# Attention and mixer kernel: weight and second-batch loads in one run on POOL ahead of casts, v's shifted copies on VectorE, first lists rearranged

## The chip, the cores and the metric

The kernel runs on one core of a Trainium2 chip. The metric is the device time of one execution in microseconds (us), of which several runs are taken. Engines are called as in the profile: PE (TensorE, matmuls), DVE (VectorE), ACT (ScalarE), POOL (GpSimd) and SP (SyncE, which here only issues DMAs). PE's clock is granted by a throttle; the profile gives it as a share of full speed.

## The reference

Eight batches, eight heads, 576 positions, 64 elements a head. First attention with a window of 32 to either side and 8 global positions, which see and are seen by all; then a mixer over tokens (576 to 256 and back) and one over channels (512 to 1536 and back).

```python
scores = scale * np.matmul(q, k.transpose(0, 1, 3, 2))
mask = np.abs(pos[:, None] - pos[None, :]) <= window
mask = mask | is_global[:, None] | is_global[None, :]
scores = np.where(mask, scores, -1000000000.0)
attn = softmax(scores)          # row maximum taken off, sum + 1e-09
x = np.matmul(attn, v)          # heads side by side: B, S, 512
xt = x.transpose(0, 2, 1)
h = np.maximum(xt @ w_tok1, 0.0) @ w_tok2
u = x + h.transpose(0, 2, 1)
h2 = np.maximum(u @ w_ch1, 0.0) @ w_ch2
return u + h2
```

## The kernel before

**Stages of a batch.** q and k come in as float32 (`lq`, `lk` for the first 512 positions, `lqr`, `lkr` for the last 64) and are cast to float16 (`cast_qk`, L384 and L381). PE transposes them (`T`, L398, and `TR`, L425), and DVE copies the result out of PSUM (`TEq`, `TEk`, L404 and L410; `TRE`, L436). `S_` (L456) makes the scores in the window, `SX` their exponentials on ACT (L468), `SM` the masks on DVE (L474, L479). `GK`, `LX`, `LM` serve the global keys, `OG` (with the DVE result `rf`, L542) the global queries. `PV` multiplies by v (L654, L663) and divides by the row sums (L676, L677), giving `x16s`. `M1` and `M2` (L690, L710) are the token mixer; `M3` transposes u by DMA (`uT`, L727; for the last tile `uTl`, L730). `M4` (L738) and `M5` (L764) are the channel mixer: 12 and 8 units of about 0.87 and 1.3 us per batch. An output tile `osb` (L768) is added on DVE and sent by SP (L769).

**Shifted copies.** A tile of v holds 128 positions, a query tile 64. So there is a second copy of v, shifted by 64 rows (`vod`, made by `v_odd`, L371 and L372: two copies over 64 partitions). For batch 0, v arrives in float32 (`lv`) and is cast by POOL (`castv`, L376); later batches are loaded and cast at once by five DMAs from POOL (`load_v16`, L359).

**Order.** All engines' orders are those of the program. There is no automatic scheduling. Batch 0's attention and token mixer come from a list written out by hand at the end of the function (L882 to L1016), in which the weight loads (`load_w1`, L247, `load_w1l`, `load_w2`, `load_wc1`, `load_wc2`, L263; float32 to float16, so all on POOL) and the loads of batch 1's q and k (`load_qk1`, on POOL too) are placed. After that, period b runs the dense units (`M4`, `M5`) of batch b, with the sparse work of batches b+1 and b+2 between them. In period 0 the list is `period_0` (L821 to L835): a `D` in it stands for one dense unit. Period 1 merges the list of `sparse2` (L779) with the dense units by planned durations; from period 2 on `first_half` and `second_half` repeat. 

**Queues.** SP's queue holds batch 0's q, k and v, the outputs, the transposes and the q and k loads of batch 2 and on (`load_rest`, L120, `load_qk`, L116), in that order of issue: a load behind an output waits until that output's tile is there. In `period_0` of before, the loads for batch 2 stand ahead of batch 1's last masks and its `OG`. POOL's queue holds, for batch 1, the casts of q and k, `v_odd(1)`, and the gathers of the global rows.

**Buffers.** q, k (float16), v, `vod` and the transposed q and k are double, by b % 2; `lq` and `lk` are single, so their loads wait for the casts of the batch before. PSUM has three pools: `pss` (two buffers), `psv` (one), `psm` (two, also of the dense units).

Of the kernel before, what the change touches and what calls it, by code (L numbers as in the profile page):

```python
# [15 lines left out]
P = 128  # L16
# [28 lines left out]
def kernel(  # L45
# [72 lines left out]
    def load_rest(b):  # L118
        for ten, dst in ((q, lqr), (k, lkr)):
            (nc.scalar if b == 0 and ten is q else nc.sync).dma_start(out=dst.rearrange("p i d -> p (i d)"), in_=rest_src(ten, b))  # L120
# [12 lines left out]
    for p in range(NP):  # L133
        load_qk(0, slice(2 * p, 2 * p + 2))
        if p == 0:
            load_rest(0)
        if p == 2:
            load_v0(0)
# [19 lines left out]
    def qk_pads(i):  # L158
        nc.gpsimd.memset(kTs[i][:, :, 0:WIN], 0.0)
        nc.gpsimd.memset(kTs[i][:, :, WIN + S :], 0.0)  # L160

    qk_pads(0)
    nc.gpsimd.memset(qTs[0][:, :, :, 0:NG], 0.0)
# [113 lines left out]
    nc.gpsimd.memset(lv[0:WIN, 0], 0.0)  # L277
    nc.gpsimd.memset(lv[P - WIN : P, NT - 1], 0.0)
# [10 lines left out]
    def v_rows(i):  # L289
        nc.gpsimd.memset(vsh[i][0:WIN, 0], 0.0)  # L290
        nc.gpsimd.memset(vsh[i][P - WIN : P, NT - 1], 0.0)
# [102 lines left out]
    def T(b, p):  # L394
        pT = (psm if b == 0 else pss)([P, 2, 512], F16, name=f"pT_{b}_{p}")
# [23 lines left out]
    def TR(b):  # L419
        pr = (psm if b == 0 else pss)([P, 2, 4, NP * 16], name=f"pr_{b}")  # L420
# [85 lines left out]
    def GK(b):  # L506
        s = st[b]
        ps = (psv if b == 0 or b > 2 else pss)([P, 2, 512], name=f"gk_{b}")
# [23 lines left out]
    def OG(b):  # L532
        s = st[b]
        ps = (psv if b > 2 else pss)([P, 2, VW], name=f"og_{b}")
# [13 lines left out]
    def OG0(p):  # L548
        s = st[0]
        if p == 0:  # L550
# [48 lines left out]
    def M1_0(p):  # L599
        s = st[0]  # L600
        if p == 0:
# [43 lines left out]
    def PV(b, tau):  # L645
# [4 lines left out]
        ps = (pss if b > 2 and tau % 2 else psv)([P, 2, 512], name=f"pv_{b}_{tau}")  # L650
# [128 lines left out]
    def sparse2():  # L779
# [7 lines left out]
        for p in range(NP):  # L787
# [33 lines left out]
    def period_0():  # L821
# [6 lines left out]
        u += [D, lambda: SM(n, 2), lambda: GK(n), s2(n, 3), D, lambda: (load_rest(m), load_qk(m, slice(0, H)))]  # L828
        u += [lambda: SM(n, 3), D, lambda: OG(n), D, lambda: PV(n, 0), D, lambda: PV(n, 1), D]
        u += [lambda: PV(n, 2), lambda: [M1(n, ch) for ch in range(2)], lambda: PV(n, 3), D]  # L830
        u += [lambda: PV(n, 4), lambda: M1(n, 2), D, lambda: [M1(n, ch) for ch in range(3, NT)], *c2]
        u += [lambda: (M2(n, 0), M3(n, 0)), lambda: (M2(n, 1), M3(n, 1)), lambda: (M2(n, 2), M3(n, 2))]
        u += [lambda: (load_v16(m), v_odd(m)), lambda: globals_(m), lambda: TR(m)]
        u += [lambda p=p: t(m, p) for p in range(NP)]
# [46 lines left out]

    W(10)  # L882
    indices()
    W(20)
    consts()
    cast_qk(0, 0, 0, A)
    cast_qk(0, 1, 0, A)
    cast_qk(0, 0, None, V)
    T(0, 0)
    gather(0, (1,))  # L890
    masks_c()
    TEq(0, 0, V)
    TEk(0, 0, A)
    cast_qk(0, 0, 1, A)
    cast_qk(0, 1, 1, V)
    S_(0, 0, 0)
    SX(0, 0, 0)
    gather(0, (0,))
    v_ones(0)
    v_rows(0)  # L900
    nc.gpsimd.memset(w1l, 0.0)
    T(0, 1)
    cast_qk(0, 0, 2, V)
    masks_b()
    TEk(0, 1, A)
    TEq(0, 1, A)
    cast_qk(0, 1, None, A)
    S_(0, 1, 0)
    cast_qk(0, 1, 2, G)
    TR(0)  # L910
    masks_d()
    SX(0, 1, 0)
    G(out=g16[1][0], in_=g32[1][0])
    T(0, 2)
    TRE(0, (1,), V)
    TRE(0, (0,), A)
    castv(0)
    S_(0, 1, 1)
    TEq(0, 2, V)
    TEk(0, 2, A)  # L920
# [3 lines left out]
    G(out=g16[0][0], in_=g32[0][0])  # L924
    load_w1()
    load_w1l()
    load_w2()
    cast_qk(0, 1, 3, V)
    gather_t(0)
    SX(0, 0, 1)  # L930
    S_(0, 2, 0)
    GTE(0)
    GKE(0)
    T(0, 3)
    SX(0, 2, 0)
    v_odd(0, slice(0, 2), nc.vector)
    S_(0, 2, 1)
    TEk(0, 3, A)
    TEq(0, 3, V)
    SX(0, 2, 1)  # L940
    GQ0()
# [116 lines left out]
```

The softmax here doesn't subtract the row's maximum and nothing guards it: scores larger than these inputs give would overflow.

## Time and profile before

| | us |
|---|---|
| median of 5 runs | 351.67 |
| lowest and highest run | 349.37 and 352.43 |
| the profiled execution | 348.58 |
| its span | 346.7 |
| PE busy | 310.5 (90%) |
| DVE busy | 187.5 (54%) |
| ACT busy | 154.0 (44%) |
| POOL busy | 95.9 (28%) |

The lines shown below are from one profiled execution. The span is what the trace covers; the execution's own time is some 2 us longer. The mean granted clock was 0.984. Numbers such as L398 are lines of the kernel before; a bracket at the end of a line tells how long the engine stood idle just before and what ended that.

Two lines of the page show where PE is less than busy, in 40 slices of 8.67 us:

```profile
PE   5599689783999999799989999899989999999993
DMA  7899959999939873948194914968101221052012
```

A digit is the busy share in tenths (9 stands for 90% or more). PE's low digits are nearly all in the first ten slices, that is in the start-up and in period 0; the DMA engines are nearly full in the first slices.

### The profile page before, as it was taken

How to read it: one execution, taken by the hardware profiler on the slowest of the kernel's cores; microseconds unless marked ns; L12 is line 12 of the kernel's file. 1: busy time of each engine (PE TensorE's matmuls, PEld its weight loads, DVE VectorE, ACT ScalarE, POOL GpSimd, SP SyncE). 2: the span in 40 equal slices, each digit the busy share in tenths (PEclk: the TensorE clock that was granted, in tenths of full speed). 3: DMA queues.
4: the chain of work that ended last, by engine and by line, in shares of the span. 5: the costliest groups of instructions: out<-in, count | busy, mean ns of one | idle time of the engine just before them, and what ended most of it. 6: DMA issues, size and time to landing. Idle time of an engine off the chain costs nothing.

```text
span 346.7 us, 8081 instructions
## 1 busy us (share of the span) xinstructions
PE 310.5 (90%) x3431; PEld 166.8 (48%) x3431; DVE 187.5 (54%) x380; ACT 154.0 (44%) x276; POOL 95.9 (28%) x125
## 2 busy tenths in 40 slices
PE   5599689783999999799989999899989999999993
PEld 5368344432346544444445644454545545444641
DVE  5588166548653875576647464566656364231021
ACT  4554463042757145463465444554555433403600
POOL 8995292856415101520052002510000000000000
PEclk9699999999899999999999999999999999999999
DMA  7899959999939873948194914968101221052012
GB/s 219 195 149 225 230 78 149 300 144 121 228 82 89 253 173 47 87 151 223 70 97 121 218 62 79 85 211 169 62 2 30 62 93 33 0 119 79 0 74 80
DMA packets 82022, 42.37 MB, mean 122 GB/s; under 512 B 56578, under 2 KB 76674, under 8 KB 81986
## 3 DMA queue, kind: packets, MB, share of 16 engines
q1 hardware_dynamic: 43944, 31.20, 33.2%
q0 software_dynamic: 37904, 10.52, 28.8%
q8 instruction: 27, 0.44, 0.5%
q10 hardware_dynamic: 138, 0.13, 0.1%
q14 instruction: 9, 0.07, 0.1%
HBM read 36.11 MB, written 9.44 MB: 131 GB/s over the span
## 4 chain that ended last, share of the span: by engine, by line
PE 69%; DMA 11%; DVE 8%; POOL 6%; issue 2%; SPq 1%; ACT 1%; POOLq 0%; ACTq 0%
PE op L764 25%; PE b1p L738 20%; DMA lk<-in_k_dram 6%; PE a1p L690 4%; PE hp L710 4%; PE pv L654 3%; PE b1lp L751 3%; PE pv L663 2%; PE s L456 2%; DMA vsh<-in_v_dram 2%; PE pT L398 2%; DMA uT<-u 1%; DVE x L677 1%; DVE e_all L479 1%; DMA lv<-in_v_dram 1%
## 5 line engine op out<-in xcount | busy, mean ns | idle before, releaser
L738 PE MATMUL b1p<-uT,wc 128*128 128x512 f16 x384 | 95.9, 383 | 2.1 <-DMA uT<-u 2.1
L741 ACT ACTIVATE b<-b1p 128x512 f16<-128x512 f32 x96 | 57.0, 598 | 91.4 <-PE b1p L738 91.3
L764 PE MATMUL op<-wc,b 128*128 128x512 f16 x384 | 89.8, 380 | 0.0
L468 ACT ACTIVATE e_all<-s 128x544 f16<-128x544 f32 (+1 forms) x64 | 41.2, 687 | 40.2 <-issue 32.3
L359 POOL DMA_DIRECT2D vsh<-in_v_dram x35 | 29.5, 862 | 98.3 <-PE pv L663 91.3
L764 PEld LDWEIGHTS <-b 128*128 128x128 f16 x384 | 35.2, 98 | 38.9
L738 PEld LDWEIGHTS <-wc 128*128 128x128 f16 x384 | 34.4, 98 | 39.0 <-issue 4.0
L768 DVE TENSOR_TENSOR osb<-u,op 128x512 f32<-128x512 f16 x32 | 22.0, 687 | 54.4 <-PE op L764 52.2
L404 DVE COPY qT<-pT 128x512 f16<-128x512 f16 x31 | 21.3, 687 | 15.4 <-PE pT L398 15.3
L479 DVE TENSOR_TENSOR e_all<-e_all,bandm 128x616 f16<-128x616 f16 x56 | 27.9, 539 | 1.0
L676 DVE RECIPROCAL rr<-pv 128x8 f32<-128x8 f32 (+1 forms) x35 | 7.3, 207 | 36.7 <-PE pv L663 36.7
L715 DVE TENSOR_TENSOR u<-x,hp 128x1024 f16<-128x1024 f16 x14 | 17.0, 1220 | 18.6 <-PE hp L710 18.6
L677 DVE TENSOR_TENSOR x<-pv,rr 128x512 f16<-128x512 f32 (+1 forms) x35 | 24.2, 691 | 1.2
L456 PE MATMUL s<-qT,kT 64*64 64x136 f16 (+2 forms) x704 | 18.4, 220 | 5.5 <-ACT kT L410 1.3
L456 PEld LDWEIGHTS <-kT 64*64 64x64 f16 x704 | 11.8, 108 | 19.8 <-issue 14.2
L398 PE MATMUL pT<-ident,qn 128*128 128x128 f16 x128 | 12.8, 224 | 8.9 <-DVE kT L436 7.2
L654 PE MATMUL pv<-rf,lf 128*64 128x264 f16 x126 | 19.1, 287 | 1.9 <-DVE rf L542 0.9
L710 PE MATMUL hp<-a,w 128*128 128x512 f16 x72 | 18.8, 379 | 1.6 <-ACT a L694 1.2
L371 POOL COPY vod<-vsh 64x2112 f16<-64x2112 f16 (+1 forms) x8 | 14.2, 1780 | 17.7 <-DMA vsh<-in_v_dram 17.5
L410 DVE COPY kT<-pT 128x512 f16<-128x512 f16 x28 | 19.1, 681 | 0.0
L663 PEld LDWEIGHTS <-e_all 128*64 128x64 f16 x504 | 18.5, 111 | 1.1 <-issue 1.0
L663 PE MATMUL pv<-vsh,e_all 128*64 128x66 f16 x280 | 18.8, 194 | 0.0
(170 smaller groups left out, 374.3 us busy)
## 6 DMA issues: line engine op xcount, KB each, us to landing
out_dram<-osb SPq DMA_DIRECT2D x32, 256.0 KB
lq<-in_q_dram SPq DMA_DIRECT2D x6, 1024.0 KB
lk<-in_k_dram SPq DMA_DIRECT2D x6, 1024.0 KB
wc<-in_moe_w_ch_dram POOLq DMA_DIRECT2D x6, 512.0 KB, 8.5
vsh<-in_v_dram POOLq DMA_DIRECT2D x21, 128.0 KB, 4.6
vsh<-in_v_dram POOLq DMA_DIRECT2D x14, 96.0 KB, 3.4
lq<-in_q_dram SPq DMA_DIRECT2D x4, 256.0 KB
lk<-in_k_dram SPq DMA_DIRECT2D x4, 256.0 KB
```

What stands on the lines that cost most here:

```text
L359: nc.gpsimd.dma_start(out=vsh[b % 2][r0:r1, c, :, 0:D], in_=v[b, :, j0 : j0 + (r1 - r0), :].rearrange("h p d -> p h d"),)
L456: nc.tensor.matmul(ps[o, par, i0 - a : i1 - a], lhsT=kT[r, HQ * j : HQ * j + HQ], rhs=qf[r, i0:i1], start=b > 0, stop=b > 0 or j in js[-2:],)
L468: nc.scalar.activation(out=e2[:, :, a:z], in_=ps[:, :, 0 : z - a], func=AF.Exp, scale=scale)
L479: nc.vector.tensor_mul(out=e2[:, par], in0=e2[:, par], in1=bm)
L654: nc.tensor.matmul(ps[r0 : r0 + 64, hf, 0 : NP * VW], lhsT=s["lf"][:, HQ * t : HQ * t + HQ], rhs=s["rf"][:, 2 * hf : 2 * hf + 2], start=Tr ...
L663: nc.tensor.matmul(ps[r0 : r0 + 64, hf, VW * hh : VW * hh + VW], lhsT=e_all[:, h, lo : lo + HQ], rhs=(vod if t % 2 else vsh)[b % 2][:, tau ...
L677: nc.vector.tensor_tensor(out=x16s[b % 2][r, tau, :].rearrange("p (f h x) -> p f h x", f=2, h=NP), in0=pq[r, :, :, 0:D], in1=rr[r].unsquee ...
L710: nc.tensor.matmul(ps[:, i, :], lhsT=w2[:, ch, P * tau - sh : P * tau - sh + P], rhs=s["a1"][:, ch, :], start=(ch == 0), stop=(ch == 1),)
L738: nc.tensor.matmul(ps, lhsT=wc1[:, cc, P * j : P * j + P], rhs=s["uT"][:, cc, :], start=(cc == 0), stop=(cc == 3))
L741: nc.scalar.activation(out=s["b1"][:, j, :], in_=ps, func=AF.Relu)
L764: nc.tensor.matmul(ps, lhsT=w, rhs=wc2[:, j, :], start=(j == 0), stop=(j == NJ - 1))
L768: nc.vector.tensor_add(out=osb, in0=s["u16"][:, tau], in1=ps)
```

## The change

- Memsets of pads in `kT`, `qT` and `lv` move from POOL to DVE; those of v's unused rows for batch 0 shrink to the one extra column and go to DVE.
- In the start-up the order is rearranged on all engines: constants before the first warm-up matmuls, casts for pair 0 shared between DVE and ACT, the cast of k's pair 2 from POOL to ACT, all pieces of `v_odd(0)` on DVE, the heads' order in `PV0` and behind it 1, 0, 3, 2.
- On SP the last rows of batch 0's q and k are loaded after pair 1 rather than after pair 0, and q's go through SP rather than ACT.
- On POOL, `load_w1`, `load_w1l` and `load_w2` come before the first v casts. The loads of the channel weights, of batch 1's q and k and of batch 1's v stand in one run, and only behind them and a memset of `x16s` come the casts of batch 1's q and k, which before stood between `load_wc2(0)` and `load_wc2(4)`.
- `v_odd(1)` moves from POOL to DVE, into `period_0`, ahead of `OG(1)` and behind three dense units.
- In `period_0` the q and k loads for batch 2 move behind `OG(1)` and one dense unit (in SP's queue behind three outputs rather than one); `PV` of two tiles is issued back to back, in two PSUM pools; `M1(1)` is in one piece; transposes, scores and masks of pairs 0 and 1 of batch 2 move in from `sparse2`, partly ahead of `M2(1, 2)`.
- `T`, `TR`, `GK`, `OG` and `PV` of batches 1 and 2 use other PSUM pools.

```diff
     def load_rest(b):
         for ten, dst in ((q, lqr), (k, lkr)):
-            (nc.scalar if b == 0 and ten is q else nc.sync).dma_start(out=dst.rearrange("p i d -> p (i d)"), in_=rest_src(ten, b))
+            nc.sync.dma_start(out=dst.rearrange("p i d -> p (i d)"), in_=rest_src(ten, b))
...
-        if p == 0:
+        if p == 1:
             load_rest(0)
...
     def qk_pads(i):
-        nc.gpsimd.memset(kTs[i][:, :, 0:WIN], 0.0)
-        nc.gpsimd.memset(kTs[i][:, :, WIN + S :], 0.0)
+        nc.vector.memset(kTs[i][:, :, 0:WIN], 0.0)
+        nc.vector.memset(kTs[i][:, :, WIN + S :], 0.0)
...
-    def v_rows(i):
-        nc.gpsimd.memset(vsh[i][0:WIN, 0], 0.0)
-        nc.gpsimd.memset(vsh[i][P - WIN : P, NT - 1], 0.0)
+    def v_rows(i, eng=nc.gpsimd):
+        xs = slice(D, D + 1) if i == 0 else slice(0, VW)
+        eng.memset(vsh[i][0:WIN, 0, :, xs], 0.0)
+        eng.memset(vsh[i][P - WIN : P, NT - 1, :, xs], 0.0)
...
-        pT = (psm if b == 0 else pss)([P, 2, 512], F16, name=f"pT_{b}_{p}")
+        pT = (psm if b in (0, 2) else pss)([P, 2, 512], F16, name=f"pT_{b}_{p}")
...
-        ps = (pss if b > 2 and tau % 2 else psv)([P, 2, 512], name=f"pv_{b}_{tau}")
+        ps = (pss if b != 2 and tau % 2 else psv)([P, 2, 512], name=f"pv_{b}_{tau}")
...
-        for p in range(NP):
+        for p in (2, 3):
             u += [(0.3, lambda p=p: S_(b, p, 0)), (1.8, lambda p=p: S_(b, p, 1)), (0.0, lambda p=p: SM(b, p))]
...
-        u += [D, lambda: SM(n, 2), lambda: GK(n), s2(n, 3), D, lambda: (load_rest(m), load_qk(m, slice(0, H)))]
-        u += [lambda: SM(n, 3), D, lambda: OG(n), D, lambda: PV(n, 0), D, lambda: PV(n, 1), D]
-        u += [lambda: PV(n, 2), lambda: [M1(n, ch) for ch in range(2)], lambda: PV(n, 3), D]
-        u += [lambda: PV(n, 4), lambda: M1(n, 2), D, lambda: [M1(n, ch) for ch in range(3, NT)], *c2]
-        u += [lambda: (M2(n, 0), M3(n, 0)), lambda: (M2(n, 1), M3(n, 1)), lambda: (M2(n, 2), M3(n, 2))]
-        u += [lambda: (load_v16(m), v_odd(m)), lambda: globals_(m), lambda: TR(m)]
-        u += [lambda p=p: t(m, p) for p in range(NP)]
+        u += [D, lambda: SM(n, 2), lambda: GK(n), s2(n, 3), D, lambda: SM(n, 3), D, D, D]
+        u += [lambda: v_odd(n, eng=nc.vector), lambda: OG(n), D, lambda: (load_rest(m), load_qk(m, slice(0, H)))]
+        u += [lambda: PV(n, 0), lambda: PV(n, 1), D, lambda: PV(n, 2), lambda: PV(n, 3), D]
+        u += [lambda: PV(n, 4), lambda: [M1(n, ch) for ch in range(NT)], *c2]
+        u += [lambda: (M2(n, 0), M3(n, 0)), lambda: (M2(n, 1), M3(n, 1)), lambda: globals_(m), lambda: TR(m), lambda: t(m, 0)]
+        u += [lambda: (M2(n, 2), M3(n, 2)), lambda: (load_v16(m), v_odd(m)), lambda: t(m, 1), s2(m, 0), lambda: t(m, 2)]
+        u += [lambda: SM(m, 0), lambda: t(m, 3), s2(m, 1), lambda: SM(m, 1)]
...
+    v_rows(0, nc.vector)
...
-    cast_qk(0, 1, 2, G)
...
+    cast_qk(0, 1, 2, A)
...
+    load_w1()
+    load_w1l()
+    load_w2()
...
+    v_odd(0, slice(0, 2), nc.vector)
+    v_odd(0, slice(2, 4), nc.vector)
...
-    v_odd(0, slice(4, 6), nc.gpsimd)
...
     castv(2)
     load_wc1(0)
...
     nc.gpsimd.memset(w2[:, :, S:], 0.0)
     load_wc1(4)
     load_wc1(8)
     load_qk1()
     load_wc2(0)
-    qk_pads(1)
+    load_wc2(4)
+    load_wc2(8)
     v_ones(1)
     v_rows(1)
+    load_v16(1)
     x_pads(1)
+    qk_pads(1)
     for p in (None, 0, 1, 2, 3):
         cast_qk(1, 0, p, G)
         cast_qk(1, 1, p, G)
-    load_wc2(4)
-    load_wc2(8)
-    load_v16(1)
-    v_odd(1)
     gather(1)
```

## The prediction

> **What bounds the kernel now.** I read the head of the page first: TensorE is busy 310.5 of 346.7 us, so only some 36 us in which it stands still are there to be won. Then the chain of waits, to see where it leaves TensorE:
>
> ```profile
> PE 69%; DMA 11%; DVE 8%; POOL 6%; issue 2%; SPq 1%; ACT 1%; POOLq 0%; ACTq 0%
> 26.76 15.55 DMA lk<-in_k_dram
> 50.25 8.48 DMA vsh<-in_v_dram
> 60.88 2.09 POOL vod L372
> 81.42 5.16 DMA uT<-u
> 86.72 1.88 PE b1p L738 x4
> ```
>
> From 91 us on the chain is matmuls almost throughout; before, it runs through batch 1's k load (15.55 us from issue to landing), batch 1's v and the POOL copy of it, and the transposing DMA of batch 1. So the change is priced between 0 and 88 us, and what it gains or loses there is carried to the end. The timeline shows TensorE at these places (start, length, engine, line, operation, idle before and what ended it):
>
> ```profile
> 14.60 0.61 PE L398 MATMUL pT<-ident,kn 128*128 128x128 f16 x4 [2.50 <-POOL kn L384]
> 15.67 0.90 POOL L247 DMA_DIRECT2D w<-in_moe_w_tok_dram  x1
> 38.43 0.40 POOL L381 CAST kr<-lkr 128x256 f16<-128x256 f32 x1 [3.43 <-DMA lkr<-in_k_dram]
> 42.37 0.61 POOL L384 CAST kn<-lk 128x512 f16<-128x512 f32 x1 [2.98 <-DMA lk<-in_k_dram]
> 43.03 0.40 PE L398 MATMUL pT<-ident,kn 128*128 128x128 f16 x4 [2.65 <-POOL kn L384]
> 58.40 0.37 SPq L769 DMA_DIRECT2D out_dram<-osb  x1
> 58.87 0.67 SPq L120 DMA_DIRECT2D lqr<-in_q_dram  x1
> 61.08 0.69 DVE L542 TENSOR_TENSOR rf<-og,blk 128x528 f16<-128x528 f32 x1
> 86.72 1.86 PE L738 MATMUL b1p<-uT,wc 128*128 128x512 f16 x4 [2.12 <-DMA uT<-u]
> 89.94 1.95 DVE L474 TENSOR_TENSOR eg<-e_all,egm 128x80 f16<-128x80 f16 x1 [4.52 <-ACT e_all L468]
> ```
>
> The waits to see are 2.50, 2.65 and 2.12 us. The stretches say whether DMA was full (busy us by engine, then clock, DMA share, GB/s):
>
> ```profile
> 14.00:16.00 2.00, 1.41 (x18) 0.85 (x18) 0.76 (x2) 0.04 (x1) 2.00 (x5) 0.50 0.52 117
> 16.00:18.00 2.00, 2.00 (x28) 0.78 (x20) 1.10 (x4) 1.82 (x3) 2.00 (x4) 0.52 0.65 113
> 40.00:42.00 2.00, 0.39 (x5) 0.21 (x3) 0.10 (x1) 0.60 (x1) 0.00 (x0) 1.00 0.97 179
> 86.00:88.00 2.00, 1.28 (x4) 0.43 (x4) 0.00 (x0) 0.00 (x0) 0.00 (x0) 0.55 2.17 99
> ```
>
> DMA is full up to 42 us but for a hole at 14 to 18; so 42.37, the landing of lk(1), is set by the bytes ahead of it.
>
> **What the Trainium skill says.** "TensorE: Matmul & The Clock Gate", Part 1 (the HAM clock gate): after an idle window of about 3.4 us TensorE runs at half clock, until about as long a busy one; the window runs freely. The trace agrees: 0.55 at 86 to 88 after a nearly empty stretch, while the 2.65 us wait left the clock at 1.00. "DMA: Bandwidth & Descriptors", Queues, rings and completion order: each DMA engine serves its queues in turn, packet by packet. It agrees: the transposes of 81.42 take 5.16 us at a share of 2.17 beside the v load. "GPSIMD Engine Reference", 8. Key points: POOL shares its SBUF interfaces with VectorE, and instructions with two SBUF inputs contend. The eg multiplication takes 1.95 us in the last timeline line, beside a POOL copy, and 0.19 at 58.29 beside none.
>
> **The change, part by part.**
>
> Start-up. The rearranged lists take away TensorE's 2.50 us wait at 14.60 (kn of pair 2 now comes from ACT). Memsets and small copies move to VectorE, which has 0.76 us busy in 14 to 16, so they are hidden; were they not, some 2 us of them would sit in the same slack. I take the first M4 at 32.8 instead of 34.0. That gains nothing by itself: M4 units then wait for batch 1's k.
>
> What counts is the weight load: kn's cast (0.61), a v cast (0.72), a gather's cast (0.29) and two v memsets (0.53 each) leave from ahead of it on POOL, 2.7 us, so w1 is issued at about 13.0 instead of 15.67 and the hole fills: (1-0.52)x2 + (1-0.65)x2 = 1.7 us of DMA time, of which I take 1.1 (the rest is issue pace). lk(1) lands at 41.2 instead of 42.3; bounds 40.1 (the hole wholly filled, and earlier v) and 42.6 (reordered q and rest loads cost 0.3).
>
> POOL around 42. In the instruction list of the changed kernel each POOL DMA waits for a semaphore that the eighth before it sets on landing. wc2(4) waits for wc1(0), wc2(8) for wc1(4), and the five chunks of v(1) for wc1(8), lqr, lq, lkr and lk. The casts of batch 1 stand behind them, so POOL sits in the v chunks until lk lands; before, it cast kr at 38.43 and kn at the landing. Now: 41.2 + 0.85 (issue of the last chunk, as in the L247 row) + 0.52 (memset) + 0.74 (qr, kr) = 43.3, the start of TR(1). TR 0.35, one M4 0.87 and T(1,0) 0.6 bring 45.1, where before the same point was 43.03+0.40 = 43.4: **+1.7**. The five M4 ahead of TR are done at 32.8+5x0.87 = 37.2, so TensorE stands idle for 6 us, more than the page's window. From 86.72 the half clock costs 0.82 and 0.30 on two M4 (1.86 and 1.34 us against 1.04) and 0.2 on scores: **+1.3**, bounds 0 and 2. From 45 us on all runs 3.0 later.
>
> v(1) and its shifted copies. VectorE makes them in place of POOL, where v had landed at 58.8 and the copies ended at 62.97. v(1) is issued some 5 us earlier, so its landing no longer waits. VectorE's 64x528 copies take 0.39 us in the start-up; by four times the elements the two make 3.1, with 0.2 of each counted as fixed (its smallest operations take 0.21) 1.9. I take 2.4; beside POOL's copies, where the 64x528 form took up to 0.97, up to 5. M5(0,1) begins at 56.2+3.0 = 59.2; three half-tiles of 1.3 end at 63.1; the output sum osb 0.69: 63.8; copies: 66.2; rf 0.69: 66.9; before, rf started at 61.08. TensorE does two dense units (2.6 us) in this time that it had to do later, so M1(1) ends at about 75.2 instead of 74.0: much of the delay is paid back here.
>
> Batch 2's q and k. SP issues in order, and the loads now stand behind the output of osb_2 rather than at 58.87. osb_2 ends at 67.6; the output's issue takes 0.5, so lqr goes out at 68.1, 9.2 later. Four issues 1.7 till lk starts, 2304 KB at the 310 GB/s of these loads 7.4, the outputs between 0.8, 0.4 latency: 78.4. Beside them now come the v(3) chunks, free once PV(1) has read their buffer: **+2**, bounds 0 and 4 by taking turns. lk(2) lands at 80.4.
>
> Tail of the period. Behind lk(2): cast 0.65, T 0.4, two TE 1.36, ul 0.69, two TE 1.36, T 0.4, scores 0.75, exp 0.65, scores 0.35 = 6.6, so M4(1,0) starts at 87.0. The transposing DMAs, issued ahead, are then done, so the wait of 2.12 goes; the casts and TE are late in its place. Before it started at 86.72, but now four more score groups (0.35 each, moved in from the next period) lie behind it: equal work is 86.72+1.4 = 88.1. **Sum: -1.1 us.** The later periods have matmul in the chain and the same work. Profiled execution 348.58 - 1.1 = 347.5; it stands 3.1 below the median of the runs, so the median 351.67 - 1.1 = **350.6**.
>
> **Rivals.** Cause of faster: the clock stays full at 43 us (the window falls well, -1.3) and the v(3) chunks do not disturb lk(2) (-2.0). Then -4.4: 347.3. For it: three of the old waits are removed, and 2.65 us of idling left the clock alone. Against: 6 us are nearly two windows.
>
> Cause of slower: POOL's copies for batch 2 (1.95 each) fall on VectorE's work for batch 1. v(2) is no longer behind v_odd(1) on POOL: chunks issued from 51.5 land at 60, copies 60 to 64. There VectorE masks, in L474 and L479, and begins its own copies; each that meets a POOL copy waits as eg did (1.95). Twice that is 3.9, all ahead of rf, osb_2 and so the loads: Δ +2.8, 354.5. It decides when rf starts later than 69.1, or lk(2) lands later than 83.3. For it: the last timeline line. So does the mask pair at 58.52, 2.64 us beside such a copy where the mean of the group is 0.54 each. Against: by 63.8, when VectorE begins its own copies, POOL's are nearly done.
>
> No effect: TensorE's later waits on fixed landings swallow both signs, 351.7. That the loads do not get ahead, as POOL waits on landings anyway, is part of my forecast.
>
> **How the numbers follow.** What a measurement can tell from no change is 0.5%, 1.76 us. Forecast, own range 348.6 to 353.0 (clock 0 to 2, v 0 to 4, at about half each): chance 0.42, of which 0.21 faster (it reaches beyond -1.76 at small cost), 0.17 same, 0.04 slower. Faster rival 0.28 (0.27 faster, 0.01 same). Slower rival 0.25 (0.24 slower, 0.01 same). No effect 0.05, same. Together faster 0.48, same 0.24, slower 0.28. Range 346.3 to 355.3: from 1 below the faster to 0.8 above the slower case, and one in five outside, for the landing of lk(1) (-1.1 to +1.4) and VectorE's copies (-0.5 to +2.6), which add to any case.
>
> **What would show it.** Each step has its mark: POOL issues w1 near 13; lk(1) lands near 41.2; qr's cast starts behind the x memset near 42.6, with the clock near 0.5 behind TR(1); VectorE's two vod copies sum to 2.4 and end near 66; SP issues lqr(2) near 68; lk(2) lands near 80; M4(1,0) starts near 87, without a wait for uT; the stretch behind 90 us is as long as before less the moved scores. It would be wrong if lk(1) lands past 43, if the period behind 90 us is not of matmul pace, or if the start-up ends so late that M4 units are not done by 41.

## The result and the profile after

| | before | changed |
|---|---|---|
| median of all executions, us | 351.05 (79) | 350.73 (42) |
| mean of all executions, us | 350.88 | 350.75 |
| profiled execution, us | 348.58 | 348.14 |
| ratio, 95% interval | | 1.0036, 1.0014 to 1.0058 |

The ratio leaves out executions more than 1.5% above the fastest of their own kernel; one fast execution of before (345.05) puts its limit at 350.2, so 24 of its 79 are kept against 37 of 42 of the changed kernel, and the ratio comes out above that of the means, 0.9996. Measured once more, both kernels on one chip (the run r1 below), the ratio was 0.9947 (0.9916 to 0.9977), the means 352.62 and 353.53. One comparison has the change 0.4% slower, the other 0.5% faster. I read this as no difference that these runs settle. The forecast had 1.1 us less.

A big change thus moved the time little, and the first question is what its profile looks like. In what follows X(b) is stage X of batch b, so M4(1,0) is the first unit of M4 of batch 1; qn, kn, qr and kr are the casts of `lq`, `lk`, `lqr` and `lkr`; "the global columns" are the small VectorE copy of `gT` into `qT` (L390 before, L391 in the changed kernel). The chain of waits of the changed kernel, the page's summary and three pieces of it (start, length, what):

```profile
PE 75%; DVE 11%; DMA 5%; issue 4%; ACT 2%; SPq 1%; ACTq 0%
...
36.56 4.36 PE b1p L739 x20
42.09 3.19 DVE qT L391
71.20 9.52 DMA out_dram<-osb
```

POOL has left the chain altogether, and the 15.55 us load of lk(1) with it. In its place stand a VectorE copy of 3.19 us and one DMA stretch near 71 to 81. The timeline of the changed kernel tells what these are:

```profile
12.55 0.07 DVE L291 MEMSET vsh<- 32x8 f16 x1 [3.17 <-POOL vsh L287]
14.97 0.44 PE L457 MATMUL s<-qT,kT 64*64 64x72 f16 x10 [2.17 <-ACT kT L411]
17.02 1.78 DVE L385 CAST qn<-lq 128x512 f16<-128x512 f32 x1
17.08 2.30 POOL L377 CAST vsh<-lv 128x640 f16<-128x640 f32 x3
36.40 4.52 PE L739 MATMUL b1p<-uT,wc 128*128 128x512 f16 x20
38.71 0.79 POOL L360 DMA_DIRECT2D vsh<-in_v_dram  x1 [1.22 <-DMA lk<-in_k_dram]
40.00 0.40 POOL L382 CAST qr<-lqr 128x256 f16<-128x256 f32 x1
41.80 0.62 POOL L385 CAST qn<-lq 128x512 f16<-128x512 f32 x1
42.01 3.28 DVE L391 COPY qT<-gT 128x160 f16<-128x160 f16 x1
44.60 0.62 POOL L385 CAST kn<-lk 128x512 f16<-128x512 f32 x1
46.53 0.31 PE L457 MATMUL s<-qT,kT 64*64 64x72 f16 x10 [1.65 <-DVE kT L411]
58.58 1.33 DVE L531 TENSOR_TENSOR lf<-lf,mf 128x576 f16<-128x576 f16 x1 [1.48 <-ACT lf L527]
60.43 1.33 DVE L475 TENSOR_TENSOR eg<-e_all,egm 128x80 f16<-128x80 f16 x1
63.30 0.71 DVE L372 COPY vod<-vsh 64x2112 f16<-64x2112 f16 x1
64.66 0.69 DVE L543 TENSOR_TENSOR rf<-og,blk 128x528 f16<-128x528 f32 x1
66.50 0.65 SPq L120 DMA_DIRECT2D lqr<-in_q_dram  x1
80.73 0.62 ACT L385 CAST kn<-lk 128x512 f16<-128x512 f32 x1 [3.90 <-DMA out_dram<-osb]
87.83 1.04 PE L739 MATMUL b1p<-uT,wc 128*128 128x512 f16 x4
```

And three lines of the profile of before, for the comparison:

```profile
34.04 4.52 PE L738 MATMUL b1p<-uT,wc 128*128 128x512 f16 x20
39.91 0.19 DVE L390 COPY qT<-gT 128x160 f16<-128x160 f16 x1
43.47 0.69 DVE L404 COPY qT<-pT 128x512 f16<-128x512 f16 x1 [3.36 <-PE pT L398]
```

Read from the top. VectorE stands 3.17 us at a memset of 0.07 us, since POOL has not yet written the same tile; TensorE's scores of pair 1 wait for what is queued behind it. The casts that follow on VectorE then meet POOL's casts of v: one takes 1.78 us where the same operation took 0.43 at 12.78. The first M4 starts at 36.40 instead of 34.04. POOL sits in v(1)'s last load until lk(1) has landed (38.71), then casts. While it casts, six of these casts one behind the other (41.80 to 45.22), VectorE's small copy of the global columns takes 3.28 us, where it took 0.19 in the profile of before, and TensorE waits for the copies behind it. Batch 2's loads start at 66.50, and its k is cast at 80.73 (the bracket names an output on the same queue; in the repeat below it names lk). M4(1,0) starts at 87.83, 1.1 us later than before, but with four score groups more done ahead of it (1.4 us).

The stretches of the changed kernel (busy us of PE, PEld, DVE, ACT, POOL, then clock, DMA share, GB/s):

```profile
14.00:16.00 2.00, 1.03 (x17) 0.90 (x18) 0.72 (x2) 1.67 (x4) 1.78 (x4) 1.00 0.80 158
16.00:18.00 2.00, 2.00 (x20) 0.76 (x19) 1.58 (x2) 0.80 (x2) 2.00 (x5) 1.00 1.20 174
40.00:42.00 2.00, 2.00 (x25) 0.94 (x23) 0.66 (x2) 1.19 (x2) 2.00 (x6) 1.00 1.24 204
46.00:48.00 2.00, 0.59 (x22) 0.38 (x23) 1.67 (x3) 0.62 (x1) 1.44 (x2) 1.00 2.42 154
50.00:52.00 2.00, 2.00 (x26) 0.83 (x24) 1.97 (x5) 0.44 (x1) 2.00 (x4) 0.50 0.13 22
80.00:82.00 2.00, 0.59 (x5) 0.56 (x6) 0.00 (x0) 1.27 (x3) 0.00 (x0) 0.50 1.96 192
```

The hole in the DMA at 14 to 18 is filled, and TensorE is busy at 40 to 42, where it stood idle. It now idles in part at 44 to 48, and at 78 to 82 almost wholly (0.59 us of 2 in the last line), each time followed by half clock.

### The profile page after: what moved, and what is told of

Same layout as the page of the kernel before. It is cut to its first block, busy times and chain, and to the rows that moved or that the text cites. A ratio compares the mean times of both kernels' runs of the same rounds, so it can differ in the third digit from the quotient of the medians.

```text
span 346.4 us, 8086 instructions
## 1 busy us (share of the span) xinstructions
PE 311.9 (90%) x3431; PEld 168.8 (49%) x3431; DVE 190.8 (55%) x395; ACT 153.5 (44%) x275; POOL 86.6 (25%) x111
## 4 chain that ended last, share of the span: by engine, by line
PE 75%; DVE 11%; DMA 5%; issue 4%; ACT 2%; SPq 1%; ACTq 0%
PE op L765 24%; PE b1p L739 23%; PE hp L711 4%; PE a1p L691 4%; PE pT L399 4%; PE s L457 4%; PE pv L655 3%; PE b1lp L752 3%; DMA out_dram<-osb 3%; PE pv L664 2%; DMA lq<-in_q_dram 1%; DVE x L678 1%; DVE kT L411 1%; DMA lv<-in_v_dram 1%; DVE qT L391 1%
## 5 line engine op out<-in xcount | busy, mean ns | idle before, releaser
L405 DVE COPY qT<-pT 128x512 f16<-128x512 f16 x30 | 20.6, 686 | 14.4 <-PE pT L399 14.3
L480 DVE TENSOR_TENSOR e_all<-e_all,bandm 128x616 f16<-128x616 f16 x56 | 24.3, 476 | 1.0
L411 DVE COPY kT<-pT 128x512 f16<-128x512 f16 x30 | 20.4, 681 | 1.3 <-PE pT L399 0.8
L399 PE MATMUL pT<-ident,qn 128*128 128x128 f16 x128 | 13.9, 237 | 7.2 <-DVE kT L437 6.3
L399 PE MATMUL pT<-ident,kn 128*128 128x128 f16 x128 | 14.3, 242 | 4.6 <-ACT kn L385 4.0
```

The costliest lines, as they stand in the source:

```text
L399: nc.tensor.transpose(out=pT[:, ti, P * i : P * i + P], in_=n[b % 2][:, i, 2 * p : 2 * p + 2, :], identity=ident)
L480: nc.vector.tensor_mul(out=e2[:, par], in0=e2[:, par], in1=bm)
```

## The experiments

Two marks show where in the kernel a difference arises: the start of the first M4 (end of the start-up) and of M4(1,0) (end of period 0). Each comes from one profiled execution, and that can lie well off the mean of its kernel (341.23 against 345.56 us in f2, 356.82 against 350.34 in g1), so a mark alone settles nothing. For the two kernels that were profiled twice the stretch between the marks agrees within 1.3 us (changed and r1) and 0.1 us (e3 and r2). It is also not free of the start-up: loads in flight land when they land, so a late first M4 makes the stretch shorter. Kernels with the old period 0 (before and h3) do 1.4 us less ahead of the second mark. "Mean" is over all executions (their number), beside the mean of before measured with it; the ratio is the comparison's, with its interval. Most kernels have only 6 executions, which spread over 3 to 15 us.

| kernel | first M4 | M4(1,0) | between | mean | before | ratio |
|---|---|---|---|---|---|---|
| before | 34.04 | 86.72 | 52.7 | | | |
| changed | 36.40 | 87.83 | 51.4 | 350.75 (42) | 350.88 | 1.0036 (1.0014 to 1.0058) |
| e1 global columns first | 38.09 | 87.60 | 49.5 | 350.11 (22) | 350.35 | 0.9956 (0.9927 to 0.9985) |
| e2 loads early | 42.15 | 87.00 | 44.9 | 349.24 (22) | 350.35 | 1.0008 (0.9981 to 1.0036) |
| e3 casts first | 35.92 | 82.95 | 47.0 | 347.41 (6) | 350.35 | 0.9818 (0.9758 to 0.9879) |
| e4 old start-up list | 34.83 | 90.55 | 55.7 | 351.87 (22) | 350.35 | 1.0068 (1.0035 to 1.0102) |
| f1 memsets late | 32.91 | 91.55 | 58.6 | 351.51 (14) | 352.48 | 0.9963 (0.9922 to 1.0004) |
| f2 casts first, loads early | 35.93 | 80.24 | 44.3 | 345.56 (6) | 352.48 | 0.9809 (0.9745 to 0.9873) |
| f3 all four | 36.97 | 84.40 | 47.4 | 345.70 (6) | 352.48 | 0.9766 (0.9713 to 0.9819) |
| f4 casts first, memsets late | 36.16 | 84.07 | 47.9 | 344.66 (6) | 352.48 | 0.9703 (0.9640 to 0.9766) |
| g1 columns first, v(2) on VectorE | 42.97 | 93.33 | 50.4 | 350.34 (7) | 353.52 | 0.9886 (0.9838 to 0.9934) |
| g2 f2 and v(2) on VectorE | 35.45 | 84.80 | 49.4 | 347.46 (6) | 353.52 | 0.9810 (0.9754 to 0.9866) |
| g3 old start-up, casts first | 34.50 | 80.28 | 45.8 | 343.64 (6) | 353.52 | 0.9650 (0.9573 to 0.9727) |
| g4 casts first, v(1) on POOL | 36.36 | 84.69 | 48.3 | 350.40 (6) | 353.52 | 0.9887 (0.9813 to 0.9962) |
| h1 g3, columns first, loads early | 33.99 | 80.64 | 46.7 | 341.95 (6) | 353.71 | 0.9665 (0.9618 to 0.9711) |
| h2 g3, v(1) on POOL | 35.55 | 84.53 | 49.0 | 346.42 (6) | 353.71 | 0.9795 (0.9746 to 0.9844) |
| h3 new start-up, old period 0 | 35.11 | 87.31 | 52.2 | 350.77 (6) | 353.71 | 0.9845 (0.9763 to 0.9927) |
| h4 g3, wc2 ahead of casts | 34.77 | 83.07 | 48.3 | 345.07 (6) | 353.71 | 0.9764 (0.9714 to 0.9814) |
| r1 changed again | 35.83 | 88.51 | 52.7 | 352.62 (22) | 353.53 | 0.9947 (0.9916 to 0.9977) |
| r2 casts first again | 39.12 | 86.13 | 47.0 | 350.71 (6) | 353.53 | none given; of means 0.992 (0.980 to 1.002, by resampling) |

**First four: one part of the changed kernel each.**

e1:

```diff
-        u = [D, D, D, D, D, lambda: TR(n), D, lambda: globals_(n), lambda: t(n, 0), D]
+        u = [lambda: globals_(n), D, D, D, D, D, lambda: TR(n), D, lambda: t(n, 0), D]
```

> Edit: the VectorE copy of the global columns of batch 1 (3.28 us beside POOL's casts in the changed kernel, 0.2 elsewhere) moves from behind TR(1) to the head of period 0, before POOL's casts begin. Theory A (the loss sits in that one VectorE copy): it takes 0.2 to 0.5 us, TensorE's idle stretches at 44 to 48 us shrink from 2.5 to under 1 us, the half clock behind them goes, and M4(1,0) starts 2.5 to 3.5 us earlier than 87.8; ratio to before 0.993 to 0.997. Theory B (POOL's casts hold up VectorE whatever it does): the next VectorE operation, the TR or TE copies, takes the stall, M4(1,0) within 0.7 us of 87.8; ratio 1.001 to 1.005.

The copy took 0.19 us and no idle stretch followed at 44 to 48, as theory A had it. Between the marks it is 1.9 us less, short of its 2.5 to 3.5; M4(1,0) itself is where theory B had it, as the start-up ended 1.7 us later. So this edit shows the copy to be part of the loss at most. The rest was lost further on, in the timeline of this kernel:

```profile
57.98 1.94 POOL L372 COPY vod<-vsh 64x2112 f16<-64x2112 f16 x1 [2.52 <-DMA vsh<-in_v_dram]
58.45 1.52 DVE L475 TENSOR_TENSOR eg<-e_all,egm 128x80 f16<-128x80 f16 x1
59.98 1.94 POOL L373 COPY vod<-vsh 64x2112 f16<-64x2112 f16 x1
60.01 2.63 DVE L480 TENSOR_TENSOR e_all<-e_all,bandm 128x616 f16<-128x616 f16 x2
```

POOL's copies for batch 2 fall on VectorE's masks of batch 1: 1.52 and 2.63 us, where the same lines take 0.19 and 0.87 earlier in this execution. That is 3.1 us ahead of `rf`.

e2:

```diff
-        u += [D, lambda: SM(n, 2), lambda: GK(n), s2(n, 3), D, lambda: SM(n, 3), D, D, D]
+        u += [D, lambda: SM(n, 2), lambda: GK(n), s2(n, 3), D, lambda: (load_rest(m), load_qk(m, slice(0, H))), lambda: SM(n, 3), D, D, D]
...
-        u += [lambda: v_odd(n, eng=nc.vector), lambda: OG(n), D, lambda: (load_rest(m), load_qk(m, slice(0, H)))]
+        u += [lambda: v_odd(n, eng=nc.vector), lambda: OG(n), D]
```

> Edit: batch 2's q and k loads go back ahead of SM(1,3), so on SP behind one output instead of three. Theory A (the end of period 0 hangs on the landing of lk(2)): SP issues them near 61 instead of 66.5, lk lands at 73 to 76 instead of 80.6, TensorE's 4.0 us wait for kn goes, M4(1,0) starts at 83 to 85 instead of 87.8; ratio to before 0.991 to 0.997. Theory B (the transposing DMAs of batch 1, 77 to 83, or the copies out of PSUM take its place): M4(1,0) at 86.5 to 88; ratio 1.000 to 1.005.

The wait for kn went, and it is 6.6 us less between the marks, but the profiled execution began with a start-up 5.8 us longer, so the two are not comparable in M4(1,0), which lies in theory B's band for this reason. In time it is 1.1 us below before by the means and level by the ratio: what the early loads are worth by themselves is left unsettled. In the start-up the same instructions ran at half speed for longer. The recorded clock says 1.00 in both kernels at this place, the durations don't; the transposes of pair 2 in this kernel and then in the changed one:

```profile
18.65 0.61 PE L399 MATMUL pT<-ident,qn 128*128 128x128 f16 x4
```

```profile
18.86 0.40 PE L399 MATMUL pT<-ident,qn 128*128 128x128 f16 x4 [0.40 <-DVE qn L385]
```

e3:

```diff
     load_qk1()
     load_wc2(0)
-    load_wc2(4)
-    load_wc2(8)
     v_ones(1)
     v_rows(1)
-    load_v16(1)
     x_pads(1)
     qk_pads(1)
     for p in (None, 0, 1, 2, 3):
         cast_qk(1, 0, p, G)
         cast_qk(1, 1, p, G)
+    load_wc2(4)
+    load_wc2(8)
+    load_v16(1)
     gather(1)
```

> Edit: on POOL the casts of batch 1's q and k go back ahead of the second and third part of wc2 and of v(1), as before the change. Theory A (POOL's place is not what costs: M4 units still run when the casts are done): TR(1) still starts at 40.5 to 41.5, v(1) lands later but by 58, M4(1,0) within 1 us of 87.8; ratio to before 1.001 to 1.006. Theory B (my prediction's: POOL standing in the v chunks costs about 1.7 us and more with the clock): M4(1,0) 1.5 to 3 us earlier; ratio 0.994 to 0.999.

Theory A, that POOL's place cost nothing because TensorE was still at M4 units, is wrong; B is right in sign. But the time did not come from an idle TensorE ahead of TR(1), as B had it: T(1,0) is 5.7 us behind the first M4 in both kernels. It comes from VectorE, as its timeline shows:

```profile
41.53 0.49 DVE L391 COPY qT<-gT 128x160 f16<-128x160 f16 x1
...
56.30 0.20 DVE L475 TENSOR_TENSOR eg<-e_all,egm 128x80 f16<-128x80 f16 x1
56.52 0.87 DVE L480 TENSOR_TENSOR e_all<-e_all,bandm 128x616 f16<-128x616 f16 x2
```

With the casts first, POOL is done with them at 42, and the copies for batch 2, now behind a later v load, run at 61.7 to 65.6 us, beside VectorE operations that read PSUM and kept their 0.69 us. The 3.28, 1.33 and 1.33 us of the changed kernel are 0.49, 0.46 and 0.20. The edit also moves the loads of v(1) and wc2, so it tests POOL's order as a whole.

e4: the start-up list, its memsets and loads of before, with POOL's run from `load_qk1` on, period 0 and pools of the change.

```diff
     load_qk1()
     load_wc2(0)
-    qk_pads(1)
+    load_wc2(4)
+    load_wc2(8)
     v_ones(1)
     v_rows(1)
+    load_v16(1)
     x_pads(1)
+    qk_pads(1)
     for p in (None, 0, 1, 2, 3):
         cast_qk(1, 0, p, G)
         cast_qk(1, 1, p, G)
-    load_wc2(4)
-    load_wc2(8)
-    load_v16(1)
-    v_odd(1)
     gather(1)
```

> Edit: the start-up list, its memsets and its loads are those of before; POOL's run from batch 1's loads on, period 0 and the PSUM pools are those of the change. Theory A (the new start-up list gives 2.4 us away on TensorE, but lands lk(1) 3 us earlier, and both hang together): first M4 at 34.0 instead of 36.4, lk(1) lands at 41 to 42.5, TensorE idles until 43 or later, half clock follows; M4(1,0) at 87 to 90; ratio to before 1.000 to 1.008. Theory B (the start-up list is a plain loss): M4(1,0) at 85 to 86; ratio 0.994 to 0.998.

Theory A, though M4(1,0) is 0.6 us past its band: TensorE waits 4.14 us for qr ahead of TR(1) at 43.49, half clock follows, and the copy of the global columns takes 3.33. With an early end of the start-up POOL's wait is what my forecast described. The execution profiled, at 354.06 us, is one of this kernel's slower ones.

**Second four.** f1 moves the memset:

```diff
-    v_rows(0, nc.vector)
...
     cast_qk(0, 1, 3, V)
+    v_rows(0, nc.vector)
```

> Edit: the two small memsets of v's extra column that the change moved to VectorE go behind the last casts of batch 0 in the start-up list; in the changed kernel VectorE stands 3.17 us at the first of them until POOL's memset of the same tile is done. Theory A (the new start-up list is late because of this wait): VectorE casts q of pair 2 at about 9.4 instead of 12.8, TensorE's 2.2 us wait at 12.8 to 15.0 shrinks to under 1 us, the first M4 starts at 33 to 35 instead of 36.4; but POOL's casts still come at 40, so TensorE then stands idle ahead of TR(1) and little reaches the end: mean of all executions within 1.5 us of the changed kernel's 350.8. Theory B (other waits, as the arrival of q and k, hold the start-up): first M4 within 0.7 us of 36.4, no change in time.

```profile
9.30 0.43 DVE L385 CAST qn<-lq 128x512 f16<-128x512 f32 x1
...
14.18 0.42 DVE L385 CAST qn<-lq 128x512 f16<-128x512 f32 x1
...
42.77 3.33 DVE L391 COPY qT<-gT 128x160 f16<-128x160 f16 x1
```

```profile
32.91 4.52 PE L739 MATMUL b1p<-uT,wc 128*128 128x512 f16 x20
41.29 0.43 PE L426 MATMUL pr<-ident,qr 128*64 128x64 f16 x8 [3.86 <-POOL qr L382]
...
41.99 1.89 PE L739 MATMUL b1p<-uT,wc 128*128 128x512 f16 x4
```

VectorE's timeline and then TensorE's, of this kernel. The cast of pair 2 comes at 9.30 instead of 12.78 and the first M4 at 32.91: the forecast's 32.8. And then what the forecast said next: a wait of 3.86 us for POOL, and 1.89 us for an M4 at half clock. The gain of 3.5 us ends there: POOL's copies then meet VectorE's masks (1.80 us for eg, 2.63 for the pair behind it), M4(1,0) is 3.7 us later than in the changed kernel, and the mean is within 1 us of its mean. Nor is the early first M4 sure: f3 and f4 have this start-up list too, VectorE casts pair 2 as early in them (9.47 and 9.30), but after half clock from about 26 to 33 us their first M4 starts at 36.97 and 36.16.

f2 is e2 and e3 together; f3 is e1, e2, e3 and f1; f4 is e3 and f1.

> Edit: POOL's casts of batch 1 first, as in the earlier run, and batch 2's loads ahead of SM(1,3) as well. Theory A (both ends are real and add up): lk(2) lands before 72, no wait for its cast, M4(1,0) at 79 to 81.5 against 83.0 with the casts alone; mean 343 to 345, ratio to before 0.978 to 0.985. Theory B (the landing is hidden behind the transposing DMAs or the copies out of PSUM): M4(1,0) within 1 us of 83.0, mean 345 to 348.

> Edit: the three edits of the runs before (casts first, loads early, global columns first) and the late memsets together. Theory A (POOL's order no longer limits, so an earlier start-up reaches the end): first M4 at 33 to 35, M4(1,0) at 77 to 80, mean 340 to 344, ratio 0.970 to 0.980. Theory B (TensorE now waits for lk(1), which lands at 38, as it did in the kernel before): the earlier start-up is lost in a wait ahead of T(1,0), mean within 1 us of that of casts and loads alone.

> Edit: POOL's casts first and the late memsets, loads of batch 2 where the change has them. Tells the value of casts first with more executions than the 6 of the earlier run (mean 347.4, median 345.4). Theory A (POOL's place costs about 4 us): mean 344 to 347, ratio 0.980 to 0.990, M4(1,0) at 81 to 83.5. Theory B (the earlier run was a lucky draw of clock states): mean 348.5 to 351, ratio above 0.993.

f2 met A in its marks (M4(1,0) 80.24), its mean is 0.6 us above A's band and in B's. f3 missed A's bands but for the ratio: in the profiled execution half clock at 26 to 34 took the earlier start-up away again, and then M4(1,0) waited 2.52 us for uT; its mean is that of f2, as B had it. f4's mean is at the low end of its band, its ratio below it, its M4(1,0) later than expected. Beside f1, from which only POOL's order differs and with which it was measured, its mean is 6.8 us lower (340.42 to 348.46 against 347.95 to 354.60): this speaks for a cost of POOL's place, not for luck. r2, below, is weaker.

**Third four.** g1 (on e1) and g2 (on f2) take batch 2's copies from POOL:

```diff
-        u += [lambda: PV(n, 4), lambda: [M1(n, ch) for ch in range(NT)], *c2]
+        u += [lambda: PV(n, 4), lambda: (load_v16(m), v_odd(m, eng=nc.vector)), lambda: [M1(n, ch) for ch in range(NT)], *c2]
...
-        u += [lambda: (M2(n, 2), M3(n, 2)), lambda: (load_v16(m), v_odd(m)), lambda: t(m, 1), s2(m, 0), lambda: t(m, 2)]
+        u += [lambda: (M2(n, 2), M3(n, 2)), lambda: t(m, 1), s2(m, 0), lambda: t(m, 2)]
```

> Edit: the changed kernel with the global columns first, and with batch 2's two shifted copies of v taken from POOL (58 to 62 us, beside VectorE's masks of pair 3) to VectorE, behind PV(1,4). Theory A (POOL's 1.95 us copies stall VectorE there: eg 1.52 for 0.19 and masks 2.63 for 0.87 in the run with global columns first, about 3 us): these go back to 0.2 and 0.9, rf starts 2 to 3 us earlier after the first M4 (24 instead of 26.6), M4(1,0) 48 after the first M4 instead of 49.5 or less; mean 346 to 348.5, as with POOL's casts first. Theory B (casts first gains by the casts themselves): mean 349.5 to 351.

> Edit: casts first, loads of batch 2 early, and batch 2's shifted copies on VectorE behind PV(1,4). Theory A (with casts first POOL's copies already fall into the PV stretch, where VectorE reads PSUM and isn't disturbed): no further gain, mean 344.5 to 347. Theory B (the copies still cost): mean 342 to 344.

In g1's timeline the masks of pair 3 are back at 0.20 and 0.87 us, so it was POOL's copies that stalled them:

```profile
65.97 0.20 DVE L475 TENSOR_TENSOR eg<-e_all,egm 128x80 f16<-128x80 f16 x1
66.20 0.87 DVE L480 TENSOR_TENSOR e_all<-e_all,bandm 128x616 f16<-128x616 f16 x2
```

The gain in time is not shown: the profiled execution was at half clock from 12 to 39, and the mean, 350.34, lies in B's band, though before, measured beside it, took 3 us more than beside e1, so that the ratio is lower than e1's (0.9886 and 0.9956). g2 is no faster than f2. In it VectorE waits 6.39 us for batch 2's v at 74.27, as the load comes late there, and TensorE behind it 3.69: a bad place for the copies.

g3 is e4 with POOL's order of e3; g4 is e3 with these lines:

```diff
     load_v16(1)
+    v_odd(1)
     gather(1)
...
-        u += [lambda: v_odd(n, eng=nc.vector), lambda: OG(n), D, lambda: (load_rest(m), load_qk(m, slice(0, H)))]
+        u += [lambda: OG(n), D, lambda: (load_rest(m), load_qk(m, slice(0, H)))]
```

> Edit: the start-up list, memsets and loads of before, POOL's casts first (as before), but v's shifted copies of batch 1 on VectorE, period 0 and PSUM pools of the change. Theory A (the gain of casts first comes from period 0 and the VectorE copies, and the new start-up list is worth its earlier lk(1), 3 us): first M4 near 34.5, T of k of batch 1 waits until 42 or later, mean 347 to 349.5, slower than the casts-first runs (345.8). Theory B (the start-up list is worth nothing): mean 345 to 346.5.

> Edit: casts first, and batch 1's shifted copies back on POOL. Theory A (VectorE making them in 1.4 us beside no POOL copy is a gain): POOL copies at 53 to 57 stall the masks of pairs 2 or 3 by 1 to 2 us, but they end before OG; v lands at 52, so rf is at most 1.5 us later or up to 1 us earlier; mean 346 to 348. Theory B (that VectorE copy is the cost that casts first hides): mean 343 to 345.

g3 is before with nothing changed but period 0, its PSUM pools, v(1)'s copies on VectorE and the place of batch 1's pads on POOL. I expected it slower than the runs with the new start-up list; its mean is below both bands, and its ratio, 0.9650, the lowest of all, within the interval of f4's. In its timeline on TensorE:

```profile
73.74 0.40 PE L398 MATMUL pT<-ident,kn 128*128 128x128 f16 x4 [1.81 <-ACT kn L384]
...
80.28 1.87 PE L738 MATMUL b1p<-uT,wc 128*128 128x512 f16 x4 [0.68 <-DMA uT<-u]
```

k of batch 2 is ready 7.7 us earlier than in the changed kernel (73.74 against 81.41), and M4(1,0) starts 7.6 us earlier. g4's mean is above both bands, and slower than all others with casts first except r2's; POOL's copies put the last mask pair at 2.65 us.

**Last six.** What was open then: whether POOL's loss stands alone, which load makes it, and what in period 0 gains. h1 is g3 with e1 and e2. h2 is g3 with g4's lines. h4 is g3 with the two wc2 loads ahead:

```diff
     load_wc2(0)
+    load_wc2(4)
+    load_wc2(8)
     v_ones(1)
...
-    load_wc2(4)
-    load_wc2(8)
     load_v16(1)
```

h3 is the changed kernel with `period_0`, the loop in `sparse2` and the PSUM pools of before, and

```diff
     for p in (None, 0, 1, 2, 3):
         cast_qk(1, 0, p, G)
         cast_qk(1, 1, p, G)
+    v_odd(1)
     gather(1)
```

> Edit: start-up list of before and POOL's casts first (as in the fastest run so far, mean 343.6 against 353.5 of before), period 0 of the change, and batch 2's loads early and the global columns first. Theory A (lk(2), which lands 2.2 us late for its cast in that run, is what ends period 0): M4(1,0) at 77 to 79.5 instead of 80.3; ratio to before 0.955 to 0.965. Theory B (the transposing DMAs, which M4(1,0) waited for by 0.68 us, take its place): M4(1,0) at 79.5 to 81, ratio 0.963 to 0.975.

> Edit: as the fastest run so far, but batch 1's shifted copies of v on POOL, as before. Theory A (VectorE's copies, 1.4 to 1.7 us beside no POOL work, are a good part of the gain): POOL copies at 56 to 60 stall the masks of pair 3 and the loads come later; M4(1,0) 2 to 4 us after 80.3, ratio to before 0.972 to 0.985. Theory B (the list of period 0 makes the gain alone): M4(1,0) at 80 to 81.5, ratio 0.962 to 0.970.

> Edit: the complement: start-up list, memsets and POOL's run of the change, but period 0, the PSUM pools and batch 1's shifted copies on POOL as before. Theory A (the change is a gain in period 0 and a loss of the same size in POOL's run, which cancel): slower than before, M4(1,0) at 93 to 98 against 86.7, ratio 1.015 to 1.035. Theory B (the loss exists only together with the new list of period 0): ratio 0.995 to 1.010.

> Edit: as the fastest run so far, but the second and third load of wc2 ahead of POOL's casts; only v(1)'s loads stay behind them. Theory A (it is v(1)'s five loads, each behind the landing of an earlier POOL DMA up to lk, that hold the casts; wc2 has its slots free by 31 us): kr is cast when it lands, near 37, as without; ratio to before 0.960 to 0.975. Theory B (any load ahead of the casts delays them or lk): casts of kn 2 us later, ratio 0.980 to 1.005.

h1 has the lowest mean, 341.95, and a narrow spread (340.36 to 343.05); against before 0.9665, so it beats both kernels. Whether it beats g3 (0.9650) these runs don't tell, and its M4(1,0) is no earlier: theory B for the marks. h2: with v(1)'s copies back on POOL the mean is 7.3 us below that of before, in g3 it is 9.9, so the copies are worth about a quarter of the gain by the means, and two fifths by the ratios (0.9795 and 0.9650). In h4 qr and kr are cast as they land (32.59, 36.63) and kn at 39.35, so it is v(1)'s five loads that hold the casts, not wc2. Its ratio is just above A's band, its mean 1.4 us above g3's.

h3 lies below both bands and refutes my theory A. The start-up list with POOL's run, under the old period 0, is no loss: 350.77 against 353.71 in the mean; its second mark is 0.6 us later than that of before. There too POOL's casts are late (TensorE waits 2.77 us at 42.40) and the columns' copy takes 3.34. POOL's copies of v(1) still strike a mask pair (2.63), but that of pair 0, with time to spare ahead of `rf`. So the loss is no fixed price of POOL's run; in these runs it shows only together with the new period 0.

> The changed kernel once more, beside before and the casts-first kernel on one chip, since before was at 350.3 to 353.7 in the other calls. Theory A (gain in period 0 and loss by POOL's run cancel): mean 350 to 352.5, ratio of means to before 0.992 to 1.002; Theory B (the change as a whole is a loss): ratio of means above 1.003.

> The changed kernel with POOL's casts first once more, beside the changed kernel on the same chip. Theory A (POOL's run ahead of the casts costs 3 to 6 us): mean 345 to 347.5, that much below the changed kernel; kr is cast near 36, the global columns' copy takes under 0.7 us. Theory B (the earlier run was luck): within 1.5 us of the changed kernel.

The copy of the global columns in r1 and then in r2:

```profile
42.02 3.45 DVE L391 COPY qT<-gT 128x160 f16<-128x160 f16 x1
```

```profile
44.73 0.19 DVE L391 COPY qT<-gT 128x160 f16<-128x160 f16 x1
```

r1 repeats the stall and the marks; its ratio of means, 0.9974, is in A's band, its mean just above it. r2's span between the marks, 47.0, is that of e3 to 0.1 us, 5.7 below r1's. Its mean meets neither band: it is only 1.9 us below r1's, with 6 executions from 341.9 to 355.8, and its start-up ended at 39.12. In time the pair is inconclusive; the stretch between the marks agrees with e3 and the changed kernel.

## Why the prediction was wrong

What happened to the expected gain: period 0 as the change has it gains, g3 shows 9.9 us in the mean (343.64 against 353.52) and 8.3 between the marks on equal work. POOL's order and the start-up list take it back. The means of kernels that share the new period 0 and v(1)'s copies on VectorE, less the mean of before measured with each:

| | POOL's run as changed | casts first |
|---|---|---|
| old start-up list | +1.5 (e4) | -9.9 (g3) |
| new start-up list | -0.1, -0.9 (changed, r1) | -2.9, -2.8 (e3, r2) |
| new list, memsets late | -1.0 (f1) | -7.8 (f4) |

With the old start-up POOL's run costs all of the gain (11 us; 55.7 and 45.8 between the marks). With the new one it costs 2 to 3 in the mean, 4.4 to 5.7 between the marks. And with the casts first the new start-up costs some 7 us, of which the late memsets bring back about 5. So either of the two takes most of the gain by itself, and the loss of one hides that of the other. (The kernels of the right-hand column, and only they, have 6 executions each, so its sizes are rough.) The forecast had the signs of period 0, -4.1, and of POOL with the clock, +3.0, right and both too small; for the start-up it had no loss at all.

By its steps:

- *Start-up, first M4 at 32.8.* **This step failed**: the moved memsets were called hidden. One waits 3.17 us for POOL's memset of the same tile, with the casts and copies of pair 1 and 2 queued behind it on VectorE. Behind the wait, the casts meet POOL's v casts (1.78 us for one). 36.40 was measured, and 35.1 to 43.0 in the ten other profiles with this list, where the old list has 34.0 to 35.6. f1 shows 32.91 without that wait, f3 and f4 36.97 and 36.16. I had priced the memsets' work and not their wait. In the changed kernel itself the step does not set the time, since f1 is no faster; it does once the casts come first.
- *lk(1) lands at 41.2.* The hole was filled, as said, and w1 was issued at 14.25, not 13.0. POOL resumes behind lk at 38.71, 2.5 us earlier than forecast: the size was off.
- *POOL in v(1)'s loads until lk lands, +3.0.* **The cost of this step was misplaced**: the order is right (38.71, the memset, qr at 40.00). But with the late M4 units there was no idle time for it to make: the forecast's +1.7 was -0.7 (T(1,0) done at 42.7 against 43.4), and the +1.3 for the clock did not arise there. In f1 and e4, where the start-up ends early, both arise.
- *What took its place* was not in the forecast at that spot: POOL's casts beside VectorE's copy of the global columns, +3.1 us on VectorE, two TensorE waits of 1.65 and 0.88, half clock at 49 to 52. This is the mechanism of the slower rival, in another place. The rival's own place is there too, at half its price: lf and eg take 1.33 each, 2.0 us more than undisturbed; `rf` at 64.66 is short of the 69.1 from which it would decide.
- *v(1)'s copies 2.4 us on VectorE.* 1.41 were measured; both ends of my bound were too high. The linear scaling from the small copies was wrong.
- *Batch 2's loads at 68.1, lk(2) at 80.4.* 66.50 and 80.7: late start rightly seen, the transfer 14.2 instead of 12.3 us beside v(3), within its bound.
- *Period 0, -4.1.* **This term was mis-sized**, its mechanism right: in g3, which has neither POOL's run nor the new start-up, `rf` starts at 59.52, batch 2's loads at 61.43, and k of batch 2 is cast at 73.06. The forecast less its 3.0 has 63.9, 65.1 and 77.4: it was four us late at `rf` already; behind that its steps were near (11.6 us from load to cast for 12.3, 7.2 to M4(1,0) for 6.6).
- *Tail 6.6, M4(1,0) at 87.0, no wait for uT.* 7.1, at half clock, 87.83, no wait. On equal work -0.3 instead of -1.1.

So the end of the sum was near for the profiled execution (-0.4 in its own time), and this is luck, by errors that cancel: the start-up 3.6 too early, the landing 2.5 too late, a clock loss expected in one place and met in another. A sign forecast from such a sum is not worth much, and the measured sign is not settled either.

Two readings in the working were loose, neither worth 0.1 us: the row of L247 says 0.90 us, not 0.85, and a transpose of 5.16 us shows that it was slow beside the v load, not in which order the packets went.

What stays open: why the old period 0 hardly suffers from POOL's run (h3), why the start-up stays longer at half speed in some executions, and the worth of the loads' place by itself. Having ACT make the copy of the global columns, out of POOL's way, was not tried.

## What to carry to other kernels

Before moving a small operation to an idle engine, ask what it waits for and what stands behind it: a 0.07 us memset cost 3.2 us of VectorE. Loads pulled ahead of casts on one in-order engine delay the casts until the loads ahead have landed (here 38.71), and then shift everything that engine does later onto other work: check which VectorE operations will lie beside POOL's copies. Test the parts of a large edit separately, and in pairs: here one part was worth 3.5% by its ratio (2.8% by the means), each of two others took most of it back, and taking away only one of these two showed little (f1) or a third (e3).

## What the runs showed of the hardware

- A VectorE copy of 128x160 between SBUF tiles took 3.28, 3.33, 3.33, 3.34 and 3.45 us in the five profiles (changed, e4, f1, h3, r1) where a long row of POOL casts lay beside it, and 0.18 to 0.62 where the casts were nearly done or it came clear of them. In e2 and g1 the row met the last masks of the start-up instead (L305): 3.52 and 3.81 us for two, 0.49 in the changed kernel. The Trainium skill ("GPSIMD Engine Reference", 8. Key points) names the shared interfaces and ties the contention to two-port modes or two SBUF inputs of VectorE; no trace shows the mode of this one-input copy. The price here is that of about six POOL casts in a row, not of one: the copy of the changed kernel ends at 45.29, the last cast at 45.22. Copies out of PSUM are not stalled: in before four of them kept 0.68 and 0.69 us beside such a row (43.47 to 46.07).
- TensorE's half clock can last far longer than the gap that began it. "TensorE: Matmul & The Clock Gate", Part 1, has full clock return after about 3.4 us of work. In g1 the clock was 0.50 from 14 to 38 us, with TensorE busy 2.00 of 2 us in nine of twelve stretches, three of which stand below; the measurement decides, though what the throttle counts as work no trace shows. In 14 profiles with the new start-up list the first M4 started anywhere from 32.9 to 43.0 us, the two latest (e2 and g1) being those that ran longest at half speed; in six with the old list it started from 34.0 to 35.6.

```profile
20.00:22.00 2.00, 2.00 (x20) 1.00 (x18) 1.28 (x4) 1.21 (x2) 1.34 (x4) 0.50 0.79 103
28.00:30.00 2.00, 2.00 (x52) 1.71 (x47) 1.84 (x8) 0.00 (x0) 0.39 (x1) 0.50 1.23 203
36.00:38.00 2.00, 2.00 (x25) 1.84 (x24) 1.21 (x3) 0.00 (x0) 1.60 (x2) 0.50 1.06 302
```
